# Sliding-window attention and Fourier mixing: crossbar transposes in one piece, crossbar transposes for four more chunks, and the masks of two head pairs moved from TensorE to VectorE

## The chip, the cores and the metric

The kernel runs on one core of a Trainium2 chip. The metric is the device time of one execution in microseconds (us), as the median of several runs.

The engines have these names in the profile: PE is TensorE (matrix multiply), PEld its weight loads, DVE is VectorE, ACT is ScalarE, POOL is GpSimd, and SP is SyncE, which here does nothing but issue DMAs. The crossbar is the way of a DMA that transposes 2-byte data from one place in the on-chip memory to another (`dma_start_transpose`).

## The reference

There are two stages. The first is attention over q, k, v of shape (batch 4, heads 8, sequence 768, head size 64). A query at position i sees the keys j with 0 <= i - j < 96 (the local band) and the 8 first keys (the global ones). Each score gets a bias that depends on head and distance:

```
scores = scale * q @ k.T
bias   = -slope[h] * dist          # dist = i - j in the band, 96 for the global keys
a      = softmax(where(keep, scores + bias, -1e9))
x      = a @ v                     # then heads side by side: (4, 768, 512)
```

The second stage mixes by Fourier transforms and ends in a two-layer network:

```
u   = x + real(fft(fft(x, axis=1), axis=2))
un  = (u - mean(u)) / sqrt(var(u) + 1e-6)
out = u + relu(un @ w_ch1) @ w_ch2      # w_ch1 512 x 2048, w_ch2 2048 x 512
```

## The kernel before

**Tiles.** Two heads are worked on together as a head pair `hp` (four a batch); `n = 4 * b + hp` counts head pairs over all batches, 0 to 15. The second stage works on chunks of 256 sequence rows: chunk `c = 3 * b + pr`, three a batch, twelve in all.

**Attention of a head pair.** q and k are loaded into `qs` or other staging tiles in fp32, cast to fp16 (`qk16`), and transposed to `TT` (profile name `qkT`), so that the head dimension lies on the partitions. In batches 0 and 1 TensorE transposes (`trans`, L527) and an engine copies the result out. In batches 2 and 3 (`b >= FB`) the crossbar does it (`trans_dma`, L499): four DMA transposes of 64 partitions by 768 elements each (L506), one for each half `a` of the partitions and each parity `t` of the position. The loads go through three `qs` buffers, so a load waits for the cast of the head pair before. q and k come with one DMA each, v with two, one for each parity (L343).

Then come three score units a head pair (`score`, L542, g = 0, 1, 2): 128 keys against the 256 queries that their band reaches, for two blocks of keys and both heads, so four matmuls with 64 rows each (L564). In batches 0 and 1 two matmuls ahead of them (L554, L559) put the bias and the mask into the accumulator: scaled identity `sid` times the distance table `dist`. ScalarE then writes the exponential straight to `ex` (L587). In batches 2 and 3 these two matmuls are left out: ScalarE writes the exponential to a buffer `er` (L584), and VectorE multiplies it by the mask `mk` = exp(-slope * dist) into `ex` (L599). The masks are made by ScalarE (L1309), two a head pair, after batch 1's attention. The global keys have their own matmuls (`glob`, L643), on keys gathered in `kG` by two small GpSimd copies a head pair (L493). `av` (L691) multiplies the exponentials with v, and VectorE normalizes.

**Between the stages.** x goes to DRAM and back in another row order (`bounce`: writes L730, read L738; ScalarE issues them for b > 0). VectorE folds x, `y_unit` (L892) and `u_unit` (L972) do the transforms by matmul, and GpSimd mirrors some results (L940).

**Second stage of a chunk.** u is scaled to fp16 `un` and transposed to `UNT` (profile name `unT`): for chunks 0 to 6 by TensorE (`nt_unit`, eight transposes at L1063, then one copy by ScalarE or VectorE, L1071 or L1073), for chunks 7 to 11 by the crossbar (`nt_dma`, L1043), two DMA transposes a chunk (L1048). There are two `unT` buffers: the transpose of chunk c waits until the ph of chunk c - 2 is done. ScalarE squares `un` in place once `unT` is there (L1031). `ph_unit` (L1091) is the first layer in 8 units a chunk (eight matmuls of 256 columns each), its relu by ScalarE or VectorE (L1097, L1098). `pg_unit` (L1114) is the second layer, eight groups of four matmuls a chunk for chunks 0 to 7; from chunk 8 on it is L1195 with fewer products.

**Order.** The class `Plan` writes the order of all instructions before the kernel runs. It keeps an estimated clock for each engine, estimated costs for each operation, and tokens for what each step needs. TensorE draws from four streams (`MIX` transforms and u transposes, `ATT` attention, `PH`, `PG`): it takes the unit that can start first by the estimates, in the first two streams from the next ten. Work of other engines is emitted when its estimated start comes, each with a rank. Each engine then executes its list strictly in that order; on SP one list holds loads, crossbar transposes and stores of results (L1128, L1269), and a transpose that waits for its input holds back what stands behind it. Score tiles in the accumulator memory come from a ring `xx` of two banks, and while batches 0 and 1 are worked on also from two banks `C` and `D`. These two are then given to the ph and pg rings: the token `("CD",)` opens the ph units when the last user of C and D is done. `BANKS(b)` says which rings a unit may use.

## Time and profile before

| what | us |
|---|---|
| median of 7 runs | 269.84 (269.17 to 271.75) |
| the profiled execution | 270.58 |
| its span, first to last instruction | 268.8 |
| outside of the span | 1.8 |
| mean granted TensorE clock | 0.999 |
| weights w_ch1, w_ch2 have landed; loads of batch 2 begin | 71.1 |
| first score matmul of batch 2 | 106.1 |
| first ph matmul; first ph of chunk 6 (batch 2) | 54.3; 171.4 |

How to read it: a row of the timeline gives the start in us from the first instruction, the duration, engine and line, what is written and what is read, the shapes and a count. Matmuls are pipelined and their ends are modelled, so that durations of neighbours overlap; what a group costs TensorE is the distance from its start to the start of the next group. A row of the waits gives the engine and line that waited, for whom, the total in us, how often, and the longest wait. The tenths of the span have 40 slices of 6.72 us, each digit the busy share in tenths.

Of the DMAs, the crossbar transposes for q and k are issued 32 times with a median of 1256 ns on SP and land 2.4 to 6.5 us after their issue (median 3.7). Those for u are issued 10 times, 1217 ns, and land 2.4 us after.

### The profile page before, as it was taken

The page shows a single profiled execution, that of the slowest core. Times are in us where ns is not written, and L with a number is a line of the kernel's source. Part 1 is how long each engine was busy: PE and PEld are TensorE (multiplying, and loading weights), DVE is VectorE, ACT ScalarE, POOL GpSimd, SP SyncE. Part 2 cuts the span into 40 slices and gives each one's busy share as a digit, 9 for nine tenths or more (in the row PEclk, how much of TensorE's full clock was granted, in tenths as well). Part 3 has the DMA queues.
Part 4 walks back from the last instruction along what each step waited for, and adds up shares of the span by engine and source line. Part 5 has one row for each costly group of instructions (what it writes and reads, how often), then busy time and mean ns, then how long its engine had stood idle before and what let it go on. Part 6 is the DMA issues. An engine that isn't in the chain of part 4 may idle for free.

```text
span 268.8 us, 6248 instructions
## 1 busy us (share of the span) xinstructions
PE 255.7 (95%) x2540; PEld 181.4 (67%) x2540; DVE 172.6 (64%) x349; ACT 151.2 (56%) x263; POOL 60.1 (22%) x127
## 2 busy tenths in 40 slices
PE   8899899999999899999999799999999999999994
PEld 3454558577855776676675356769777668888883
DVE  3566873833399475861559957878998645525473
ACT  1479693987536737993880354896443345444300
POOL 1442398143010152321200307101100511010000
PEclk9999999999999999999999999999999999999999
DMA  7999959999589975996898896402072241511122
GB/s 202 294 291 308 295 181 234 216 216 213 125 156 256 274 159 120 217 188 131 218 153 191 171 308 151 106 2 41 0 166 110 59 97 42 81 40 41 39 82 78
DMA packets 75743, 42.03 MB, mean 156 GB/s; under 512 B 32834, under 2 KB 71746, under 8 KB 75714
## 3 DMA queue, kind: packets, MB, share of 16 engines
q1 hardware_dynamic: 68658, 32.71, 51.6%
q0 software_dynamic: 4224, 4.19, 9.3%
q10 hardware_dynamic: 2832, 4.72, 7.3%
q8 instruction: 20, 0.33, 0.6%
q14 instruction: 9, 0.07, 0.1%
HBM read 31.92 MB, written 9.44 MB: 154 GB/s over the span
## 4 chain that ended last, share of the span: by engine, by line
PE 66%; DMA 20%; SPq 4%; DVE 3%; POOL 2%; ACT 2%; issue 1%; ACTq 0%; POOLq 0%
PE ph L1091 26%; PE pg L1114 12%; DMA w<-in_moe_w_ch_dram 10%; PE pgD L1195 5%; DMA qs<-in_q_dram 5%; PE sc L564 4%; PE py L892 4%; PE pgA L1195 4%; PE pav L691 3%; DMA u<-in_v_dram 3%; PE pu L972 3%; DMA qs<-in_v_dram 2%; PE sc L559 2%; SPq L506 2%; SPq L372 2%; PE pt L527 1%
## 5 line engine op out<-in xcount | busy, mean ns | idle before, releaser
L1091 PE MATMUL ph<-unT,w 128*128 128x256 f16 x768 | 94.1, 273 | 2.7 <-ACT hT L1097 1.6
L1091 PEld LDWEIGHTS <-w 128*128 128x128 f16 x768 | 72.7, 98 | 17.1 <-issue 6.2
L1097 ACT ACTIVATE hT<-ph 128x512 f16<-128x512 f32 x78 | 46.2, 596 | 41.5 <-PE ph L1091 41.4
L1114 PE MATMUL pg<-w,hT 128*128 128x512 f16 x256 | 60.7, 379 | 0.0
L1114 PEld LDWEIGHTS <-hT 128*128 128x128 f16 x256 | 24.2, 98 | 23.4 <-issue 0.6
L587 ACT ACTIVATE ex<-sc 128x992 f16<-128x992 f32 (+2 forms) x24 | 20.8, 924 | 8.4 <-PE sc L564 8.4
L584 ACT ACTIVATE er<-sc 128x992 f16<-128x992 f32 (+2 forms) x24 | 21.6, 922 | 3.7 <-PE sc L564 3.5
L376 ACT ACTIVATE qk<-qs 128x384 f16<-128x384 f32 (+1 forms) x29 | 13.8, 525 | 14.8 <-DMA qs<-in_q_dram 5.3
L1123 DVE SCALAR_TENSOR_TENSOR u<-pg,sm,u 128x512 f32<-128x512 f32 x16 | 12.0, 747 | 12.2 <-PE pg L1114 12.2
L1098 DVE TENSOR_SCALAR hT<-ph 128x512 f16<-128x512 f32 x18 | 12.4, 690 | 10.8 <-PE ph L1091 10.8
L466 POOL CAST v<-qs 128x768 f16<-128x768 f32 x8 | 6.8, 853 | 54.4 <-DMA qs<-in_v_dram 54.4
L564 PE MATMUL sc<-qkT 64*128 64x256 f16 (+1 forms) x192 | 17.0, 262 | 2.0 <-ACT er L584 1.6
L599 DVE TENSOR_TENSOR ex<-er,mk 128x992 f16<-128x992 f16 (+2 forms) x24 | 15.0, 627 | 3.7 <-ACT er L584 3.5
L691 PE MATMUL pav<-v,ex 128*128 128x65 f16 x352 | 16.3, 193 | 1.0 <-DVE x L711 0.7
L691 PEld LDWEIGHTS <-ex 128*128 128x128 f16 x352 | 15.2, 97 | 2.4 <-DVE x L711 0.9
L564 PEld LDWEIGHTS <-qkT 64*128 64x128 f16 x192 | 5.8, 94 | 16.2 <-issue 13.9
L991 DVE SCALAR_TENSOR_TENSOR u<-pu,xr 128x512 f32<-128x512 f32 x18 | 11.7, 689 | 5.5 <-PE pu L972 3.2
L907 ACT ACTIVATE zy<-py 128x1024 f16<-128x1024 f32 (+1 forms) x12 | 10.0, 844 | 9.2 <-PE py L892 6.6
L940 POOL COPY ww<-zy 128x512 f16<-128x512 f16 x16 | 9.9, 650 | 22.7 <-PE py L892 20.6
L1038 POOL TENSOR_SCALAR sm<-sm 128x2 f32<-128x2 f32 x12 | 2.3, 193 | 56.6 <-ACT un L1031 56.5
L1031 ACT ACTIVATE un<-un 128x512 f16<-128x512 f16 x24 | 14.9, 624 | 0.0
L1195 PEld LDWEIGHTS <-hT 128*128 128x128 f16 x128 | 12.5, 98 | 1.6
(129 smaller groups left out, 381.9 us busy)
## 6 DMA issues: line engine op xcount, KB each, us to landing
out_dram<-u SPq DMA_DIRECT2D x24, 256.0 KB, 2.4
w<-in_moe_w_ch_dram POOLq DMA_DIRECT2D x8, 512.0 KB, 19.5
qs<-in_q_dram SPq DMA_DIRECT2D x9, 384.0 KB, 5.9
qs<-in_k_dram SPq DMA_DIRECT2D x9, 384.0 KB, 6.4
qs<-in_v_dram SPq DMA_DIRECT2D x16, 192.0 KB, 4.8
xr<-xd ACTq DMA_DIRECT2D x3, 768.0 KB, 5.4
u<-in_v_dram SPq DMA_DIRECT2D x5, 384.0 KB, 6.9
w<-in_q_dram SPq DMA_DIRECT2D x4, 384.0 KB, 6.5
```

What stands on the lines that cost most here:

```text
L376: A(d, s, AF.Copy)
L564: nc.tensor.matmul(pa[:, s, c0:c0 + cw], TT[n][lo:lo + 64, 1, i * P:(i + 1) * P], TT[n][lo:lo + 64, 0, i * P:i * P + cw], start=(b > 1), s ...
L584: A(mine(), cut(pa), AF.Exp, 0.0, 0.125)
L587: A(cut(expst[hp][:, :, g * 512:g * 512 + (384 if g == 2 else 512)]), cut(pa), AF.Exp, 0.0, 0.125)
L599: VT(o, mine(), m, op=ALU.mult)
L691: nc.tensor.matmul(po[:, jj, hh * 65:(hh + 1) * 65], lhsT, v16[b % 2][:, i, h, 0:65], start=(jp == 0 and a == 0), stop=(a == len(ops) - 1) ...
L1031: A(x, x, AF.Square, accum_out=MV[c][:, a, 2:3])
L1091: nc.tensor.matmul(ph[:, a * CH:(a + 1) * CH], W1[0][:, d, jb * P:(jb + 1) * P], UNT[c][:, d, :], start=(d == 0), stop=(d == ND - 1))
L1097: pl.later([("ACT", act(512), lambda: A(dst, ph, AF.Relu)), ("DVE", dve(512), lambda: V.tensor_scalar_max(dst, ph, 0.0))], [], e, [("h", c ...
L1098: ("DVE", dve(512), lambda: V.tensor_scalar_max(dst, ph, 0.0))],
L1114: nc.tensor.matmul(pg, HT[c][:, jb, t * P:(t + 1) * P], W2[0][:, jb, :], start=(jb == 0), stop=(jb == NJ - 1))
L1195: nc.tensor.matmul(o, lhs(j), rhs(j), start=(first and j == 0), stop=(j == NK - 1), skip_group_check=True)
```

## The change

1. **q and k of batches 2 and 3 in one crossbar transfer.** The four transfers of a head pair become one of 128 partitions by 1536 elements. The layout of the cast (`qk16`) changes so that one copy of 768 columns makes it, in place of two of 384. k is now loaded with two DMAs, one for each parity, as v is; q keeps one. So k's transposed blocks come out in the order that the scores want, while q's stay interleaved. The scores and the global scores of batches 2 and 3 read q through strided views (`tile_of`): the moving operand comes in runs of 64 columns. Score blocks are 256 columns wide in place of 240.
2. **u by the crossbar for chunks 3 to 11**, in one transfer a chunk in place of two; chunks 0 to 2 stay on TensorE. The layout of `unT` changes so that ph reads two runs of 128 columns.
3. **Masks of head pairs 2 and 3 of batch 1 by VectorE** (`DM`). Their scores take the path of batches 2 and 3: no bias matmuls, exponential to `er`, product with `mk`. The masks of these two head pairs are made after batch 0's last exponential in place of after batch 1's attention. The casts of v in batches 0 and 1 get buffers of their own (`v0`), so that `er` is free for this.
4. **The planner.** TensorE's clock gets 0.1 us more when a unit of scores with 64 rows follows one of another kind, or the other way round (`narrow`). Units of batch 1 may use banks C and D only while more than `KEEP` = 4 uses of them are left. Estimated costs of loads, casts and transposes are adapted.

```diff
+    def pe(self, us, after=0.0, narrow=False):
+        if narrow != self.narrow:
+            us += 0.1
+        self.narrow = narrow
...
+    KEEP = 4
...
+                                 if g and self.rings[g] and not (g in ("C", "D") and (("CD",) in self.tok or
+                                                                  "" in ring and self.left[("CD",)][0] <= self.KEEP))]
...
+    DM = ((1, 2), (1, 3))
...
-                    if w < 2:
+                    if w < 1:
                         run_dma(t.rearrange("p (m t) d -> p m (t d)", t=2), src, b, h0)
                         return
...
-            for t in range(2):
-                copy_on(on, qk16[n][:, t, w], stage[("t", n, w)].rearrange("p (h i t) d -> p t i h d", h=2, t=2)[:, t])
+            copy_on(on, qk16[n][:, w].rearrange("p n t h d -> p (n t) h d"),
+                    stage[("t", n, w)].rearrange("p (h j) d -> p j h d", h=2))
...
-        return ("xx", "C", "D") if b < 2 else ("xx",)
+        return ("xx", "C", "D") + ("",) * b if b < 2 else ("xx",)
...
+    def tile_of(n, lo, w, i, nb=1):
+
+        x = TT[n][lo:lo + 64, w]
+        if n < FB * HP or w:
+            return x[:, i * P:i * P + P].rearrange("p (t m) -> p t m", t=2)
+        if nb == 1:
+            return x.rearrange("p (i t a m) -> p i a t m", t=2, a=2, m=64)[:, i // 2, i % 2]
+        if i % 2 == 0:
+            return x.rearrange("p (i t a m) -> p i a t m", t=2, a=2, m=64)[:, i // 2]
+        o = (i // 2) * 256 + 64
+        return x[:, o:o + 384].rearrange("p (y q m) -> p y q m", y=2, m=64)[:, :, 0:3:2]
...
-            o = TT[n].rearrange("p w (i a t m) -> p a t (w i) m", a=2, t=2, m=64)[:, a, t]
-            nc.sync.dma_start_transpose(o, qk16[n][64 * a:64 * a + 64, t].rearrange("p w i h d -> p (w i h d)"))
+            nc.sync.dma_start_transpose(TT[n].rearrange("p w (j x) -> p (w j) x", x=P),
+                                        qk16[n].rearrange("p w n t h d -> p (w n t h d)"))
...
+        pem = b < 2 and (b, hp) not in DM
...
-            if b < 2:
+            if pem:
                 for s in range(2):
                     lhsT = sid[:, 2 * hp + s, :]
...
+                    if b >= FB:
+                        nb = 1 if cw == P else 2
+                        o = pa[:, s, c0:c0 + nb * P]
+                        o = o.rearrange("p (y t m) -> p y t m", y=2, t=2) if nb == 2 else o.rearrange("p (t m) -> p t m", t=2)
+                        nc.tensor.matmul(o, TT[n][lo:lo + 64, 1, i * P:(i + 1) * P], tile_of(n, lo, 0, i, nb), start=True, stop=True)
+                        continue
...
-        for a in range(2):
-            def xb(a=a):
-                if a == 0:
-                    UNT[c] = buf("unT", c, [P, ND, CH], FP16, 1)
-                nc.sync.dma_start_transpose(UNT[c][:, :, a * P:(a + 1) * P], T[("un", c)][:, a])
+        def xb():
+            UNT[c] = buf("unT", c, [P, 2, ND, P], FP16, 1)
+            nc.sync.dma_start_transpose(UNT[c].rearrange("p a d m -> p (a d) m"), T[("un", c)].rearrange("p a f -> p (a f)"))
...
-        if c >= 7:
+        if c >= 3:
             return nt_dma(c)
...
-            pl.later([("ACT", 2 * act(NM), m)], [("c", "dist"), ("x", 1, 3, 2)], 0.0, [("mk", hp)], rank=3)
+            pl.later([("ACT", 2 * act(NM), m)], [("c", "dist")] + ([] if (0, hp) in DM else [("ex", 0, 3, 2)] if (1, hp) in DM else [("x", 1, 3, 2)]), 0.0, [("mk", hp)], rank=3)
```

## The prediction

> **What bounds the kernel now.** I read the page first: busy shares, then the tenths of the span, then the chain.
>
> ```profile
> PE 255.7 (95%) x2540; PEld 181.4 (67%) x2540; DVE 172.6 (64%) x349; ACT 151.2 (56%) x263; POOL 60.1 (22%) x127
> PE   8899899999999899999999799999999999999994
> PEclk9999999999999999999999999999999999999999
> PE 66%; DMA 20%; SPq 4%; DVE 3%; POOL 2%; ACT 2%; issue 1%; ACTq 0%; POOLq 0%
> ```
>
> TensorE is busy nearly everywhere, at the full clock, so no gain can come from the clock. Is it at its peak, too? In the timeline 32 matmuls of 256 columns start at 58.74 and the next group at 62.34: 112 ns each, and elsewhere 16 take 1.75 us, 109 ns. That is a stream of columns with no gaps. So from 56 us on, a microsecond of TensorE work removed is a microsecond of time, as long as TensorE always has something ready. The second view is therefore what TensorE waited for:
>
> ```profile
> PE ph L1091 <- ACT hT L1097: 1.6, 1, 1.6
> PE sc L564 <- ACT er L584: 1.6, 1, 1.6
> PE pz L1294 <- DVE eg L1291: 1.2, 1, 1.2
> PE ph L1091 <- ACT ex L587: 1.1, 1, 1.1
> ```
>
> Three waits lie past the start: 1.1 us at 53, 1.6 at 87, 1.6 at 153. Two of them are ScalarE standing in its own queue: at 80 to 85 and at 148 to 152 it waits to issue the read of the DRAM bounce (L738), and the evacuations behind that come late.
>
> **The masks (head pairs 2 and 3 of batch 1).** The timeline of TensorE, in us from the start:
>
> ```profile
> 47.66 0.49 PE L559 MATMUL sc<-dist,sid 128*128 128x384 f16 x2
> 48.08 0.34 PE L564 MATMUL sc<-qkT 64*128 64x256 f16 x4
> 48.35 0.59 PE L559 MATMUL sc<-dist,sid 128*128 128x496 f16 x2
> 48.87 0.39 PE L564 MATMUL sc<-qkT 64*128 64x256 f16 x4
> 49.22 1.05 PE L972 MATMUL pu<-t,ww 128*128 128x128 f16 x16
> ...
> 106.10 0.39 PE L564 MATMUL sc<-qkT 64*128 64x256 f16 x4
> 106.42 1.92 PE L1091 MATMUL ph<-unT,w 128*128 128x256 f16 x16
> ```
>
> With the bias, the first score unit takes 49.22 - 48.35 = 0.87 us; a unit without it (batch 2) 0.32, and the ph group ahead of it runs 0.09 longer (1.84 against 1.75): 0.41. Saved: 0.46. The same for the 960 form (0.81 against 0.31 + 0.09: 0.41) and the 768 form (0.69 against 0.27 + 0.09: 0.33). Sum 1.20 per head pair, **2.4 us of TensorE** for two.
>
> Added: six VectorE multiplies, 2 x (0.667 + 0.653 + 0.559) = 3.8 us by the rows of L599. VectorE is full from 46 to 53 but idle for 6.7 us in four gaps between 53 and 62, and the products are first read at 73 us (av of half 1). Without that cover they would hold the two er buffers and with them the score banks. ScalarE's exps stay (989 against 997 ns). Four masks of 0.72 us move from 80-88 us to just behind batch 0's last exp; ScalarE is idle for 4.8 us between 40 and 47. So both are costed at 0. Bound: if none of the masks fits, the ph start at 54 moves by 2.9 us.
>
> **The u transposes (chunks 3 to 6).** Eight transposes start at 101.64 and the next group at 102.08: 0.44 us a chunk, **1.8 us of TensorE** for four; also four evacuations of 0.69 to 1.01 us go. Added: four crossbar issues on SP. [...] I take 1.2 + 2.4 = 3.6 us a chunk, so 2.2 us later than now, up to 6 us where loads share the queue (L506's longest landing is 6.5). Chunks 3 to 5 have cover: at 97 us TensorE has 13 of 24 pg groups of batch 0 left, 0.86 us each. Chunk 6 has none of its own; see below. The squares on ScalarE wait for the landing as well, but the factor they feed is read at the end of the chunk's pg, over 10 us on.
>
> **Wider scores.** 48 more columns per row half and head pair, in paired matmuls: 0.02 us x 8, **+0.2 us**. The moving operand is now read in runs of 64. No row shows that; the nearest, L554, reads two separate runs and costs 370 ns for 480 columns beside 375 for 496 in one. I take 0; below nothing is excluded (no fewer columns), and half rate would be 24 units x 0.21 + 0.7 for pgl = +5.8.
>
> **SP and the DMA queues.** This step adds or removes no TensorE work; it decides whether the savings stay.
>
> ```profile
> 80.81 2.71 SPq L506 DMA_TRANSPOSE qkT<-qk  x1
> ...
> 87.59 1.56 SPq L506 DMA_TRANSPOSE qkT<-qk  x1
> ...
> 93.55 2.48 SPq L506 DMA_TRANSPOSE qkT<-qk  x1
> ...
> 97.47 5.22 SPq L506 DMA_TRANSPOSE qkT<-qk  x4
> ```
>
> In batch 2 the crossbar pieces of the first head pair are spread over 17 us, because SP serves them between loads and stores that wait; its first score runs only at 106.1. One issue replaces four. 32 issues of 1.26 us become 8; I take 1.3 us each, because L1048's 512 packets of 256 bytes take no longer than L506's 384; upper end 5.0, as now. Landing: 1536 packets x 24.5 ns (their mean in the trace) / 16 engines = 2.4 us in place of 0.6, so 3.7 + 1.8 = 5.5. The first pair is then ready near 80.8 + 1.3 + 5.5 = 88. Fewer u pieces for chunks 7 to 11: 5 issues less, hidden. Casts: one of 0.84 in place of two starting 0.47 apart (0.94 the pair), nothing.
>
> Against that: k loads go to 256-byte packets, 1536 x 24.5 in place of 768 x 32.1 ns, over 16: +0.8 us x 8 = 6.5 us of all engines; the u transfers add 4 x 1024 x 24.5 / 16 = 6.3. From 70 to 170 us the queues are already busy (packets, MB, share of 16 engines):
>
> ```profile
> q1 hardware_dynamic: 39570, 15.37, 71.0%
> q10 hardware_dynamic: 1888, 3.15, 13.7%
> ```
>
> 85% plus 13% is nearly full. k's second issue (0.65 us on SP) is paid by the 24 that go.
>
> How much must batch 2 gain? TensorE's reserve is the pg groups left over from batch 1:
>
> ```profile
> 168.33 1.89 PE L1114 MATMUL pg<-w,hT 128*128 128x512 f16 x8
> 170.06 1.06 PE L972 MATMUL pu<-t,ww 128*128 128x128 f16 x16
> ...
> 171.36 1.92 PE L1091 MATMUL ph<-unT,w 128*128 128x256 f16 x16
> ```
>
> The last reserve is used at 170, just when chunk 6 is ready. If TensorE gets there 2.4 + 1.3 = 3.7 us earlier and chunk 6's transpose is 2.2 later, batch 2 has to be **5.8 us earlier**, or the saving becomes a wait. Engine time needed before its last head pair is transposed: loads 4 x (1.5 + 2.35 + 2.35) = 25, transposes 4 x 2.35 = 9, and by the same packet means the bounce 7, two u chunks and four stores 6: 47, from 71 to 118. Now the last two pairs' kG copies run at 127.6. So the gain is about 9 us: enough, by 3.
>
> **Sum.** -2.4 - 1.8 + 0.2 = -4.0. Of the waits: the masks behind the bounce read at 86.6 (1.35 us of the chain ahead of the 1.6 us wait) are halved, and batch 1 leaves its last C/D banks sooner at 53, perhaps 1 us together; but SP and ScalarE still wait for bounces on fuller queues, so I book -0.6. Total -4.6. Against its own profiled execution: 270.58 - 4.6 = 266.0 (span 268.8 to 264.2); the median of seven, 269.84, lies 0.7 below that execution: **265.2**.
>
> **Rivals.**
> *More than the work* (0.20): batch 2 comes early enough that the waits at 87 and 153 go as well: -4.0 - 3.2 = 262.6. For: both are ScalarE behind a DMA that came later than planned. Against: the read stays in ScalarE's order.
> *The saving turns into a wait* (0.13): batch 2 is only 3 us earlier, TensorE waits 2.8 before chunk 6, the other waits stay: -4.0 + 2.8, 268.6. For: 98% full queues. Against: the 9 us above.
> *Slower* (0.13): SP holds batch 2 back. The u transfer of chunk 5 waits on SP for an unT buffer until ph of chunk 3 ends, as at 173.4, where SP stood 7.9 us; there no load stood behind it, at 104 to 114 the loads of batches 2 and 3 do. Each us that batch 2 comes later adds one. Against: SP is rid of 24 issues. It decides from a gain below 5.8 - 4.0 = 1.8 us; with batch 2 one us later than now, -4.0 + 6.8 = +2.8: 272.6.
> *It does not do what it says* (0.02): runs of 64 are read at half rate, +1.2 net: 271.0.
> The forecast has 0.52.
>
> **Numbers.** 265.2; its own case holds 263.6 to 267.0. The range 261.8 to 270.0 takes in the third case and most of the second. A measurement tells about 0.5% (1.35 us) from nothing. Faster: 0.52 + 0.20 + a third of the third case = 0.76; slower nearly all of the last two, 0.14; within 0.5% the rest, 0.10.
>
> **What would show it.** The bias matmuls L559 and L554 come 24 and 12 times in place of 32 and 16, the u transposes L1063 24 times in place of 56. L506 with 8 issues near 1.3 us; the first score of batch 2 before 95 us; the reserve of pg not empty when chunk 6's ph begins; waits of TensorE not above today's. I am wrong if SP shows a long wait for ph ahead of a load, if the transfers take 5 us to issue, or if sc matmuls without bias take over 0.35 us a unit.

## The result: slower, and its profile

The changed kernel takes 274.78 us (median of 12 executions, 271.58 to 278.34) beside 269.87 for the kernel before: ratio 1.0111, interval 1.0074 to 1.0148. The forecast was 265.2, with a range up to 270.0. (Each ratio here is to executions of the kernel before taken together with that run; ratios and intervals leave out executions more than 1.5 % above the fastest of their kernel, the medians don't.) The profiled execution of after took 273.68 us, span 271.9.

The same four lines of the page as before the change, now of the changed kernel:

```profile
PE 253.0 (93%) x2504; PEld 180.1 (66%) x2504; DVE 172.4 (63%) x349; ACT 149.5 (55%) x249; POOL 64.0 (24%) x127
PE   8899899699998879799988999999999999999994
PEclk9999999999999999999999999999999999999998
PE 53%; DMA 23%; SPq 8%; DVE 5%; POOL 4%; ACT 3%; issue 2%; ACTq 0%; POOLq 0%; DVEq 0%
```

TensorE is busy for 2.7 us less, but the span is 3.1 us longer: its share falls from 95 to 93 %, and in the chain that ended last from 66 to 53 %. The tenths show where: a 6 in slice 8 (48 to 54 us, where the moved masks are), and 7s and 8s in slices 13 to 17 and 21 to 22 (82 to 116 and 136 to 150 us). As a measure of TensorE's work I count 0.4167 ns for each column of each matmul (in the trace of before, pg matmuls of 512 columns, L1114, start 216 ns apart in the median and pu matmuls of 128 columns, L972, 56: 160 ns for 384 columns; the eight of one column, L1324 and after the change L1355, which start 13 ns apart, are counted as 64 columns, 0.2 us in all and the same for both kernels; the pairs of 64-row matmuls, which start 3 to 4 ns apart, are both counted). This column work is 246.49 us before and 242.84 after: 3.65 us are gone. What is left of the time from the first matmul to the last, the lost time, rose from 17.3 to 24.0 us. Gaps over 0.3 us past 40 us, by the same count, were 6.4 us before and are 12.5 now. What TensorE waited for:

```profile
PE ph L1122 <- ACT hT L1128: 3.9, 2, 2.2
PE sc L588 <- ACT er L610: 2.1, 1, 2.1
PE pu L1005 <- POOL rev L961: 1.7, 1, 1.7
PE pz L1325 <- DVE eg L1322: 1.2, 1, 1.2
PE sc L590 <- ACT unT L1102: 1.1, 1, 1.1
```

The wait near 153 is gone; new are those at 98, 108 and 142, and the one at 87 is still there. In place of 1.1 us at 53 there are now 1.1 at 51 and 0.8 at 52. None of the four from 87 on is for a DMA by name. They are for ScalarE or GpSimd, and one has to look at what these engines stood on. ScalarE and SP around 87 us:

```profile
86.40 0.84 ACT L384 ACTIVATE qk<-qs 128x768 f16<-128x768 f32 x1 [4.49 <-DMA qs<-in_q_dram]
87.01 0.36 ACTq L771 DMA_DIRECT2D xr<-xd  x1
87.67 0.84 ACT L384 ACTIVATE qk<-qs 128x768 f16<-128x768 f32 x1 [0.43 <-DMA qs<-in_k_dram]
88.42 1.06 ACT L1128 ACTIVATE hT<-ph 128x512 f16<-128x512 f32 x2
```
```profile
79.59 0.37 SPq L380 DMA_DIRECT2D qs<-in_q_dram  x1
80.07 3.02 SPq L351 DMA_DIRECT2D qs<-in_k_dram  x2
83.18 3.79 SPq L524 DMA_TRANSPOSE qkT<-qk  x1
87.03 0.57 SPq L1159 DMA_DIRECT2D out_dram<-u  x1
87.69 1.51 SPq L351 DMA_DIRECT2D qs<-in_v_dram  x2
```

ScalarE stands for 4.49 us before a cast of q whose load SP issued only at 79.59, and the evacuation hT (the copy of a ph result out of the accumulator memory), for which TensorE waits 1.7 us at 87, is behind it in ScalarE's order. SP meanwhile spends 3.79 us on one crossbar transfer (L524, the whole head pair). The loads of v behind it start at 87.69. GpSimd stands on those at 95, and with it the mirror rows that pu needs at 98:

```profile
95.49 0.82 POOL L474 CAST v<-qs 128x768 f16<-128x768 f32 x1 [5.88 <-DMA qs<-in_v_dram]
96.26 1.17 POOL L973 COPY ww<-zy 128x512 f16<-128x512 f16 x2
```

At 108.58 ScalarE has again stood 3.42 us on a cast of q (then sc waits 2.1 us for er), and at 143 it stood 3.51 us until it could issue the read of the bounce (then ph waits 2.2).

The parts of the change did what they say. Score units without bias, here of batch 1, take the time the prediction gave them, and batch 2's first score comes at 96.15 instead of 106.1:

```profile
50.13 0.39 PE L590 MATMUL sc<-qkT 64*128 64x256 f16 x4
...
96.15 0.39 PE L588 MATMUL sc<-qkT 64*128 64x256 f16 x4
96.48 1.92 PE L1122 MATMUL ph<-unT,w 128*128 128x256 f16 x16
```

The units with q in runs of 64 columns (L588) take what the plain ones (L590) take. But the queues from 70 to 170 us are nearly full (88.7 + 12.4 %; the share is the sum of the packets' times, which can overlap, so it can pass 100), and the eight whole transfers take SP 2154 to 5711 ns each, median 3262:

```profile
q1 hardware_dynamic: 50338, 16.00, 88.7%
q10 hardware_dynamic: 1888, 3.15, 12.4%
```
```profile
L524 SPq DMA_TRANSPOSE qkT<-qk x8: 2154/3262/5711, 83.2 to 153.9; - x8
```

### The profile page after: what moved, and what is told of

The parts are those of the page before. It is cut to its first block, busy times and chain, and to the rows that moved or that the text cites. A ratio compares the mean times of both kernels' runs of the same rounds, so it can differ in the third digit from the quotient of the medians.

```text
span 271.9 us, 6121 instructions
## 1 busy us (share of the span) xinstructions
PE 253.0 (93%) x2504; PEld 180.1 (66%) x2504; DVE 172.4 (63%) x349; ACT 149.5 (55%) x249; POOL 64.0 (24%) x127
## 4 chain that ended last, share of the span: by engine, by line
PE 53%; DMA 23%; SPq 8%; DVE 5%; POOL 4%; ACT 3%; issue 2%; ACTq 0%; POOLq 0%; DVEq 0%
PE ph L1122 20%; PE pg L1145 13%; DMA u<-in_v_dram 8%; SPq L380 6%; PE pgD L1226 5%; DMA qs<-in_v_dram 4%; PE pgA L1226 4%; DMA xd<-x 3%; PE pav L724 3%; DMA w<-in_q_dram 3%; DMA qs<-in_q_dram 2%; PE pu L1005 2%; PE py L925 2%; DMA qkT<-qk 1%; DMA qs<-in_k_dram 1%
## 5 line engine op out<-in xcount | busy, mean ns | idle before, releaser
L1128 ACT ACTIVATE hT<-ph 128x512 f16<-128x512 f32 x79 | 46.9, 597 | 48.5 <-PE ph L1122 44.7
L610 ACT ACTIVATE er<-sc 128x992 f16<-128x992 f32 (+2 forms) x30 | 27.4, 922 | 6.3 <-PE sc L588 5.7
L625 DVE TENSOR_TENSOR ex<-er,mk 128x992 f16<-128x992 f16 (+2 forms) x30 | 20.1, 669 | 15.1 <-ACT er L610 15.0
L384 ACT ACTIVATE qk<-qs 128x768 f16<-128x768 f32 x14 | 11.8, 844 | 16.7 <-DMA qs<-in_q_dram 10.4
L613 ACT ACTIVATE ex<-sc 128x992 f16<-128x992 f32 (+2 forms) x18 | 15.6, 926 | 6.7 <-PE sc L590 6.4
L1154 DVE SCALAR_TENSOR_TENSOR u<-pg,sm,u 128x512 f32<-128x512 f32 x16 | 11.9, 745 | 9.9 <-PE pg L1145 9.9
L1024 DVE SCALAR_TENSOR_TENSOR u<-pu,xr 128x512 f32<-128x512 f32 x18 | 11.7, 688 | 9.4 <-PE pu L1005 4.5
L1129 DVE TENSOR_SCALAR hT<-ph 128x512 f16<-128x512 f32 x17 | 11.7, 690 | 6.7 <-PE ph L1122 6.1
L513 POOL COPY kG<-qkT 64x8 f16<-64x8 f16 x32 | 9.7, 302 | 24.5 <-DMA qkT<-qk 20.6
L474 POOL CAST v<-qs 128x768 f16<-128x768 f32 x8 | 7.6, 954 | 30.3 <-DMA qs<-in_v_dram 30.3
L940 ACT ACTIVATE zy<-py 128x1024 f16<-128x1024 f32 (+1 forms) x11 | 9.4, 867 | 8.3 <-PE py L925 8.2
L1226 PEld LDWEIGHTS <-hT 128*128 128x128 f16 x128 | 12.5, 98 | 1.6
L942 DVE CAST zy<-py 128x512 f16<-128x512 f32 (+1 forms) x8 | 6.6, 824 | 10.8 <-PE py L925 6.7
```

The lines of the kernel that those rows point to most:

```text
L384: A(d, s, AF.Copy)
L610: A(mine(), cut(pa), AF.Exp, 0.0, 0.125)
L613: A(cut(expst[hp][:, :, g * 512:g * 512 + (384 if g == 2 else 512)]), cut(pa), AF.Exp, 0.0, 0.125)
L625: VT(o, mine(), m, op=ALU.mult)
L1128: pl.later([("ACT", act(512), lambda: A(dst, ph, AF.Relu)), ("DVE", dve(512), lambda: V.tensor_scalar_max(dst, ph, 0.0))], [], e, [("h", c ...
L1154: V.scalar_tensor_tensor(UT[c][:, t, :], pg, MV[c][:, t, 3:4], UT[c][:, t, :], op0=ALU.mult, op1=ALU.add)
```

## Three theories

The program's order of each engine is written by a planner that carries an estimated time for every landing. Comparing its times with the trace: of the loads of v for the second to seventh head pair of batches 2 and 3, the plan of before has the landings at 90.2, 98.9, 107.1, 116.3, 124.5, 131.1 us, and the casts start at 92.2, 100.5, 109.3, 117.4, 126.9, 133.0, one or two us late. After: planned 90.3, 100.6, 110.6, 120.9, 130.3, 139.1, started at 95.5, 106.7, 116.5, 127.2, 136.8, 147.1, five to eight us late. (The planned times come from running the kernels' own `Plan`. A late cast can also be a consequence of waits ahead of it, but the second pair's is 5.2 us late already.)

- **O, the order.** The written order supposes landings that come 5 to 8 us too early. Casts are put on ScalarE and GpSimd ahead of evacuations that TensorE needs, and the engines stand in order on them.
- **Q, the queues.** The DMA engines are simply too full; with any order TensorE would wait.
- **M, the masks.** VectorE's six multiplies and the moved masks of ScalarE hold up TensorE.

A fourth came up in the first experiment: **C, a collision** of the first crossbar transfer of a batch with the read of the bounce.

## Experiments

**Better estimates alone (e1).** The changed kernel with the planner's numbers nearer to its trace; the arithmetic is untouched.

```diff
-                pl.later([("SP", 0.55 if w < 1 else 1.1, run)], free("qs", i) + gate, 0.0, [("ld", n, w)], lat=1.7, dma=2.0 if w < 1 else 2.67)
+                pl.later([("SP", 0.55 if w < 1 else 1.6, run)], free("qs", i) + gate, 0.0, [("ld", n, w)], lat=3.0, dma=2.2 if w < 1 else 2.9)
...
-        pl.later([("SP", 1.3, xb)], [("qk", n, 0), ("qk", n, 1)] + free("qkT", n), 0.0, [("qkT", n)], [("free", "qk", n)],
-                 lat=3.0, dma=1.5)
+        pl.later([("SP", 3.5, xb)], [("qk", n, 0), ("qk", n, 1)] + free("qkT", n), 0.0, [("qkT", n)], [("free", "qk", n)],
+                 lat=3.5, dma=1.5)
...
-                     lat=1.7, dma=2.4 if b else 2.6)
+                     lat=4.5 if b else 1.7, dma=2.4 if b else 2.6)
```

> The changed kernel, with nothing altered but the planner's estimates: loads of batches 2 and 3 land later (issue 1.6 for 1.1 us, latency 3.0 for 1.7, queue time 2.2 and 2.9 for 2.0 and 2.67), the crossbar transfer costs SP 3.5 for 1.3 us, the bounce write lands 2.8 us later. Theory O (order): TensorE's extra waits between 96 and 144 us are ScalarE and GpSimd standing in their written order at casts whose loads land 5 to 8 us later than the planner supposed; with right landings the waits of over 0.3 us shrink from 12.5 us in sum to about 7, and the time falls by 4 to 6 us, to about 268. Theory Q (queues): the transfers themselves are too many for the queues, batch 2 and 3 arrive late whatever the order, and the time stays within 1.5 us of the changed kernel's 273.

Measured: 277.0, 277.37, 279.2 and, once, 267.99 us. The waits of TensorE in the profiled execution (277.0), and SP's queue:

```profile
PE sc L588 <- DMA qkT<-qk: 8.5, 1, 8.5
```
```profile
83.47 3.35 SPq L524 DMA_TRANSPOSE qkT<-qk  x1
86.92 0.58 SPq L1159 DMA_DIRECT2D out_dram<-u  x1
87.56 5.63 SPq L351 DMA_DIRECT2D qs<-in_v_dram  x2
93.29 4.49 SPq L380 DMA_DIRECT2D qs<-in_q_dram  x1
97.88 4.73 SPq L1159 DMA_DIRECT2D out_dram<-u  x1
```

The small waits have gone, but the transfer issued at 83.47 landed after 18.7 us; the transfer issued at 83.18 in the changed kernel had landed by 89. ScalarE had issued the read of the bounce at 84.11, 0.6 us after it. Of that read's 6144-byte packets, the six that started between 84 and 87 us took 3.1 us on average, the longest 5.75; in e11 below the longest takes 0.66, in the changed kernel 1.85. SP's issues from 87.6 on take 4.5 to 5.6 us a row. Then comes a thing that I had not thought of (columns: stretch, PE busy and count, PEld, DVE, ACT, POOL, granted clock of TensorE, DMA share, GB/s):

```profile
90.00:95.00 5.00, 3.69 (x42) 3.24 (x40) 1.55 (x2) 2.22 (x3) 1.39 (x2) 1.00 1.05 110
95.00:100.00 5.00, 0.00 (x0) 0.00 (x0) 0.00 (x0) 0.00 (x0) 0.00 (x0) 0.59 1.15 151
100.00:105.00 5.00, 2.77 (x15) 1.74 (x16) 2.90 (x7) 1.30 (x2) 2.64 (x7) 0.50 0.97 202
105.00:110.00 5.00, 5.00 (x55) 3.77 (x53) 2.93 (x8) 2.63 (x5) 3.14 (x7) 0.88 1.10 194
```

TensorE's wait lasts from 93.5 to 102.2. From 95.9 to 106.2, 10.24 us, its clock is at half; the last 3.9 us of that are work at half speed. So e1 decides nothing on O by its median. Its one good execution (268.0) is 3.6 us below the fastest of the changed kernel, but one execution proves little. That a collision with the read is what held the transfer up is only suggested by their closeness in time.

**Fewer small packets (e2).** k of batches 2 and 3 loaded in one DMA with 512-byte pieces, all else in the same written order. k's rows then lie in another order than the scores suppose.

```diff
-                    if w < 1:
+                    if w < 2:
```

> The changed kernel, in the same written order, but k is loaded with one DMA of 512-byte pieces in place of two of 256-byte pieces. (Its rows then lie in another order than the scores suppose, so the output is not the reference's; all instructions and sizes are otherwise the same.) Theory Q: 6 us of all engines' queue time go, loads land 2 to 4 us earlier in the middle of the kernel, and the time falls by 3 us or more, to 270 or below. Theory O gives a smaller gain, 1 to 2 us, since landings still come 3 us or more after their planned times. If the k packets do not matter: no change within 1 us.

Measured: 272.54 us (271.5 to 274.42), ratio 1.0123 (1.0064 to 1.0183). About 2 us below the changed kernel's median; by ratio it can't be told from it. Gaps past 40 us: 9.9 of the 12.5. If the small packets cost anything, it is not what is lost. Q is not the main part.

**u of chunks 3 to 6 back on TensorE (e3), no VectorE masks in batch 1 (e4).**

```diff
-        if c >= 3:
+        if c >= 7:
```
```diff
-    DM = ((1, 2), (1, 3))
+    DM = ()
```

> The changed kernel with the u transposes of chunks 3 to 6 back on TensorE (chunks 7 to 11 stay with the crossbar). 1.8 us of TensorE work come back; 6 us of queue time go. Theory Q: 2 to 3 us of waits go, net 0 to -1. Theory O: the crossbar of u is not what is late, so the time is 1 to 2 us longer, 274.5 or so, unless the order shifts.

> The changed kernel with no masks by VectorE in batch 1 (the bias matmuls of these two head pairs back on TensorE). 2.4 us of TensorE work come back. Theories O and Q: the waits of 96 to 144 us stay, so 2 us longer, about 275. Theory M (masks): ScalarE and VectorE between 46 and 57 us are overfull with the masks, and TensorE waits for them there about as long as it saves; then the time stays within 1 us.

Measured: e3 279.1 us (277.76 to 280.21), ratio 1.037 (1.030 to 1.0439); e4 277.7 (276.26 to 280.53), ratio 1.0289 (1.0233 to 1.0345). Both are worse than the whole change. Taking a part away, and with it the work that it adds elsewhere, doesn't give its loss back: the order is written anew each time and the waits appear in other places. e4's longest is at 87.5, 4.3 us, ph behind hT on ScalarE; e3's at 149.6, 3.2 us, py behind zy on ScalarE. M in its simple form falls with e4.

**Each part alone (e5 to e8).** The kernel before with the masks, with u, with the whole transfers (and the loads of k and the casts that belong to them), and with the planner's two rules alone. The cores of the edits (e5, with all that reads `DM` and the buffers `v0`; e6, with the one-piece transfer and unT's layout; e7, with the copy, `tile_of` and the loads of k; e8, with `narrow`):

```diff
+    DM = ((1, 2), (1, 3))
```
```diff
-        if c >= 7:
+        if c >= 3:
```
```diff
-            o = TT[n].rearrange("p w (i a t m) -> p a t (w i) m", a=2, t=2, m=64)[:, a, t]
-            nc.sync.dma_start_transpose(o, qk16[n][64 * a:64 * a + 64, t].rearrange("p w i h d -> p (w i h d)"))
+            nc.sync.dma_start_transpose(TT[n].rearrange("p w (j x) -> p (w j) x", x=P),
+                                        qk16[n].rearrange("p w n t h d -> p (w n t h d)"))
```
```diff
+    KEEP = 4
```

> The kernel before with part 3 alone (masks of head pairs 2 and 3 of batch 1 by VectorE, v casts in buffers of their own; planner as before). 2.4 us of TensorE work go and no transfer changes. If the lost time of the changed kernel comes with its transfers (order or queues), the saving shows: about 267.3, TensorE's waits over 0.3 us after 40 us near 6 as before. If the masks themselves make waits (theory M): 269.5 or more.

> The kernel before with part 2 alone (u of chunks 3 to 11 by the crossbar, one transfer a chunk). 1.8 us of TensorE work go, 6 us of queue time and four SP issues come. Queues and order: waits of 1 to 3 us come back, so 269 to 271; if the u transfers are harmless: 268.

> The kernel before with part 1 alone (one crossbar transfer a head pair, k in two DMAs of 256-byte pieces, strided q). TensorE work +0.2 us. If the transfers of this part, or the order that the planner makes of their estimates, are what costs: waits in the middle of the kernel grow by 4 to 6 us, 273 to 276, with stretches of half clock in some executions. If the part is harmless by itself: 269.5 within 1.

> The kernel before with part 4 alone (0.1 us for a switch to or from 64-row matmuls, the last four uses of banks C and D kept from batch 1). No work changes; 269.5 within 1.5 if the planner's changes are harmless; over 271 if reordering by itself makes waits.

Measured, with the column work of TensorE (246.49 before) and the gaps of the profiled execution (6.4 before) beside it:

| | median us (low to high) | ratio (interval) | column work | gaps past 40 us |
|---|---|---|---|---|
| e5 masks | 270.58 (266.77 to 276.39) | 0.9991 (0.996 to 1.0021) | 244.23 | 8.0 |
| e6 u | 274.43 (274.30 to 274.98) | 1.0127 (1.0065 to 1.0189) | 244.79 | 10.5 |
| e7 q and k | 274.78 (274.32 to 276.13) | 1.0141 (1.0083 to 1.0199) | 246.81 | 7.5 |
| e8 planner | 270.21 (269.39 to 271.58) | 1.0021 (0.9997 to 1.0044) | 246.49 | 5.0 |

Masks and u each remove the work that was forecast (2.3 of 2.4, 1.7 of 1.8) and gain nothing; the planner's rules do nothing. u and the whole transfers, alone, each cost 1.3 to 1.4 %. e6 does not fit O: its casts of v start only 1.6 to 3.4 us after the plan. Its last pg group before chunk 6 starts at 164.1, chunk 6's ph at 172.9 (171.4 before), and between 166 and 173 TensorE stands 4.0 us in four gaps, most of them on VectorE's u. That looks like the prediction's rival "The saving turns into a wait": the reserve ran out before chunk 6 was ready. No run tests it further. In e7 nearly the whole loss is one place; ScalarE there, and the clock:

```profile
82.95 0.35 ACTq L758 DMA_DIRECT2D xr<-xd  x1
83.49 0.72 ACT L1329 ACTIVATE mk<-dist 128x640 f16<-128x640 f16 x1
90.28 0.84 ACT L376 ACTIVATE qk<-qs 128x768 f16<-128x768 f32 x1 [6.07 <-DMA qs<-in_k_dram]
91.03 1.07 ACT L1117 ACTIVATE hT<-ph 128x512 f16<-128x512 f32 x2
```
```profile
90.00:95.00 5.00, 3.34 (x16) 2.38 (x16) 0.69 (x1) 3.21 (x5) 0.49 (x3) 0.67 1.00 248
```

SP issued that load of k at 85.47 and it landed at 90.28; ScalarE stood 6.07 us on it with hT behind; TensorE waited 4.2 us, then ran 3.41 us at half clock. This is O at its plainest: the crossbar transfer of that cast's head pair is issued only at 97.2.

**One more staging buffer (e9), casts of q and k away from ScalarE (e10).** Both on the changed kernel.

```diff
-    NBUF = {"hT": 3, "qk": 2, "qs": 3, "qkT": 4, ...
+    NBUF = {"hT": 3, "qk": 2, "qs": 4, "qkT": 4, ...
```
```diff
-        pl.later([("ACT", act(768), lambda: cast("ACT")), ("POOL", 0.87, lambda: cast("POOL"))],
+        pl.later([("POOL", 0.87, lambda: cast("POOL"))],
```

> The changed kernel with four staging buffers for the loads of q and k instead of three; nothing else by hand (the planner writes a new order from it). Theory O (the loads land 5 to 8 us after the time that the written order supposes, and ScalarE and GpSimd stand in order on them): a load can be issued one buffer earlier, so the casts on ScalarE near 84 to 87 and 105 to 108 find their data there, and the two waits of TensorE that follow them (1.9 at 87, 2.2 at 108) shrink; the time is 269 to 272. Theory Q (the 16 DMA engines are too full from 70 to 170): the earlier issue only lengthens the queue, the landings come as late as before, and the time stays at 273 to 275.

> The changed kernel with the casts of q and k of batches 2 and 3 on GpSimd alone, so that ScalarE never stands on a load of q or k. Theory O: the waits 'ph <- ACT hT' at 87 and 'sc <- ACT er' at 108 go (together 4.1 us in the profile of the changed kernel), and GpSimd, which is 49 % busy, takes 12 more casts of 0.9 us; 269 to 271, unless GpSimd's own in-order waits (pu <- POOL rev, 1.9 us at 98) grow by as much, and then 273. Theory Q: the wait goes to the scores that lack their transposed pair, 'sc <- DMA qkT' appears, and the time stays at 273 to 275.

Measured: e9 275.3 us (272.67 to 281.56), ratio 1.0153 (1.0091 to 1.0215): no gain; the waits at 87 and 108 are gone, but 3.5 us at 94.6 (pu behind zy on ScalarE) and 2.4 at 151.7 came in their place. e10 272.84 (269.76 to 275.2), ratio 1.0054 (1.0018 to 1.009): 2 us better than the change. The waits that it was meant to remove are gone and there is no gap over 0.7 us between 71 and 150 (GpSimd was 24 % busy in the changed kernel, not the 49 % of the expectation); then GpSimd stands in its own order and TensorE loses 4.36 us at once:

```profile
PE pu L1005 <- POOL rev L961: 4.2, 1, 4.2
```

That speaks for O: the loss follows the engine that holds the casts. One more buffer (e9), with an order whose casts of v still start 0.1 to 5.2 us late, doesn't help.

**The first transfer of a batch behind the read of the bounce (e11), and that with the better estimates (e12).** The planner may place the transfer of a batch's first head pair only after the read of the previous batch's bounce. This changes places in the written order and adds no wait on a semaphore. e12 has the three edits of e1 as well.

```diff
-        pl.later([("SP", 1.3, xb)], [("qk", n, 0), ("qk", n, 1)] + free("qkT", n), 0.0, [("qkT", n)], [("free", "qk", n)],
+        pl.later([("SP", 1.3, xb)], [("qk", n, 0), ("qk", n, 1)] + free("qkT", n) + [("xr", b - 1)] * (hp == 0), 0.0, [("qkT", n)], [("free", "qk", n)],
```

> The changed kernel in which the crossbar transfer of the first head pair of a batch waits for the read of the bounce of the batch before, so that the two are never in flight together; the planner's estimates are those of the changed kernel. If the collision of a crossbar transfer with the read costs something in the changed kernel too (in the run with other estimates it took 15 us), the stretch from 82 to 95 gets calmer and the time falls by 1 to 2 us, to 271 to 273. If not, the first pair comes 2 to 3 us later, which the scores of batch 2 (first at 96, pair there at 89) don't feel: 273 to 275, unchanged.

> The changed kernel with the planner's estimates set to what its trace shows (loads of q and k 2.2 and 2.9 us of DMA time and 3.0 us until they land, 3.5 us of SP for a whole crossbar transfer, 4.5 us until the read of the bounce lands) and with the transfer of the first pair behind the read of the bounce, so that the two can't collide as they did in the run with other estimates. Theory O: the written order then fits the landings, the in-order waits of ScalarE and GpSimd fall to those of before, TensorE's waits after 40 us fall from 12.5 to some 7, no stretch of half clock is left, and the time is 267 to 269 (one execution of the earlier run without the collision took 268.0). Theory Q: the order can't help, since the data isn't there; TensorE waits for the scores' operands instead, 272 to 275.

Measured: e11 269.16 us (267.4 to 273.99), ratio 0.9974 (0.9945 to 1.0003); **e12 267.0 us (266.19 to 268.31), ratio 0.988 (0.9852 to 0.9908)**, faster than both kernels. e12's column work is that of the changed kernel, 242.84; its lost time is 18.6 us in place of 24.0. What TensorE waits for in e12, and what the casts of q and k on ScalarE and on GpSimd waited for in the changed kernel and in e12 (the group's line: count, busy, mean ns, idle before):

```profile
PE ph L1122 <- DVE hT L1129: 1.6, 1, 1.6
PE pvp L445 <- POOL v L429: 1.4, 3, 0.8
PE pz L1325 <- DVE eg L1322: 1.2, 1, 1.2
```
```profile
L384 ACT ACTIVATE qk<-qs 128x768 f16<-128x768 f32 x14 | 11.8, 844 | 16.7 <-DMA qs<-in_q_dram 10.4 <-DMA qs<-in_k_dram 6.3
L388 POOL CAST qk<-qs 128x768 f16<-128x768 f32 x4 | 3.3, 825 | 4.0 <-DMA qs<-in_k_dram 2.2 <-PE sc L590 0.9 <-DMA qs<-in_q_dram 0.9
```
```profile
L384 ACT ACTIVATE qk<-qs 128x768 f16<-128x768 f32 x11 | 9.2, 838 | 2.4 <-POOL kG L513 1.4 <-DMA qs<-in_q_dram 1.0
L388 POOL CAST qk<-qs 128x768 f16<-128x768 f32 x7 | 5.9, 845 | 20.4 <-DMA qs<-in_k_dram 19.7 <-DMA qs<-in_q_dram 0.6
```

ScalarE stands on its casts for 2.4 us instead of 16.7. Three casts have moved to GpSimd, which now stands 20.4 us on casts of q and k instead of 4.0, in places where it costs TensorE little. The bytes are nearly the same (19.0 and 19.2 MB on the two queues between 70 and 170 us; 95.0 % of 16 engines, where the changed kernel has 101.1 %), and the data is there no earlier: the casts of v of the second to sixth pair start at 94.8, 105.5, 118.1, 130.2 and 136.0 us, beside 95.5, 106.7, 116.5, 127.2 and 136.8 in the changed kernel. What has changed is the plan, which now has these landings at 92.4, 105.9, 118.4, 128.6 and 137.7. So Q falls and O holds. How much of the gain comes from the casts' other engine is not separated.

**Is it only the estimates (e13)? Which parts pay now (e14, e15)?** e13 is the kernel before with e1's estimates of loads and bounce; e14 and e15 are e12 without the masks and with u of chunks 3 to 6 on TensorE (the edits of e4 and e3).

```diff
-                pl.later([("SP", 0.55 if w < 2 else 1.1, run)], free("qs", i) + gate, 0.0, [("ld", n, w)], lat=1.7, dma=2.67)
+                pl.later([("SP", 0.55 if w < 2 else 1.1, run)], free("qs", i) + gate, 0.0, [("ld", n, w)], lat=3.0, dma=2.9)
...
-                     lat=1.7, dma=2.4 if b else 2.6)
+                     lat=4.5 if b else 1.7, dma=2.4 if b else 2.6)
```

> The kernel before with the same correction of the planner's estimates that helped the changed kernel (3.0 us and 2.9 us of DMA time for a load of q or k instead of 1.7 and 2.67, 4.5 us until the read of the bounce lands instead of 1.7); its four-part crossbar transfers stay as they are. If the gain of the corrected changed kernel is the change's own, this stays at 269 to 271, since the order of before already fits its landings to 1 to 2 us. If it is only the estimates, this one gains 2 to 3 us too, 267 to 268.

> The corrected changed kernel (267.0 us) without the VectorE masks of batch 1: TensorE has 2.3 us more work. If work is what counts once the waits are gone, 269 to 270; if the masks' waits eat their work even now, 267.

> The corrected changed kernel (267.0 us) with u of chunks 3 to 6 transposed on TensorE again: 1.7 us more TensorE work, four transfers fewer. If work is what counts, 268.5 to 269; if the transfers' 3.6 us of latency before a chunk's first product costs as much as it saves, 267.

Measured: e13 270.92 us (269.24 to 271.52), ratio 1.0026 (1.0001 to 1.0052): the estimates give the kernel before nothing. **e14 265.69 (265.3 to 266.15), ratio 0.9846 (0.9804 to 0.9888)**: without the masks it is 1.3 us faster still by the medians (0.9 by the ratios, whose intervals overlap), though TensorE has 2.3 us more work (245.11). e15 269.96 (267.69 to 274.41), ratio 0.998 (0.9952 to 1.0007): u by the crossbar is worth 3.0 us by the medians (2.7 by the ratios), more than its 1.7 us of work; the rest may be the order, which is written anew here too. So M is true in another form: once the order fits, the masks of batch 1 eat what they save. e12's waits of TensorE from 40 to 75 us, where these masks are multiplied, and e14's:

```profile
PE pvp L445 <- POOL v L429: 1.1, 2, 0.8
PE sc L590 <- ACT unT L1102: 1.1, 1, 1.1
PE pgl L676 <- ACT er L610: 0.5, 1, 0.5
```
```profile
PE sc L579 <- ACT eg L689: 0.4, 1, 0.4
PE ptu L1094 <- DVE u L1033: 0.3, 1, 0.3
```

From 40 to 80 us TensorE does no columns for 3.5 us in e12 and for 1.0 in e14. The other 2.7 us of their difference in lost time (18.6 against 13.4) lie later, most of it between 120 and 140 us.

**The transfer by itself (e16).**

> Not the computation (the output is zeros): transfers by themselves on otherwise idle queues, each round joined before the next: a whole 128x1536 crossbar transfer, the same as four pieces, the 768 KB read of the bounce in packets of 6144 bytes on ScalarE's queue, a 384 KB load in pieces of 256 bytes, and pairs of them. If a crossbar transfer and the read hinder each other by themselves, the pair takes far longer than the two one after the other (alone some 4 and 4 us; together over 12). If the collision in the run with other estimates needed the full queues, the pair takes 4 to 8 us, the sum at most.

Rounds, each joined by VectorE before the next, of these four (W, P, R, L) and of sums of them:

```diff
+    def whole():
+        nc.sync.dma_start_transpose(TT, qk)
+    def pieces():
+        for n in range(4):
+            a, t = n // 2, n % 2
+            nc.sync.dma_start_transpose(TT[:, 6 * t:6 * t + 6, 64 * a:64 * a + 64], qk[64 * a:64 * a + 64, 768 * t:768 * t + 768])
+    def read():
+        nc.scalar.dma_start(XR, xd.rearrange("(m r) d -> m r d", r=6))
+    def load():
+        nc.sync.dma_start(L.rearrange("p (h r d) -> p h r d", h=2, r=6), lsrc[:, 0:2])
```

From issue to landing, us: W 3.6 to 3.7 (SP's issue 1.27 to 1.42); P 6.3 from the first issue to the last landing (four issues of 1.2); R 4.4 to 4.6, with an L beside it, because these rounds ran side by side; W behind an L 4.3 to 4.5, and its issue then takes 2.4 to 2.8; W with R 6.4 to 6.9, and R then 5.0 to 5.3 (in the rounds with all three W takes 5.2 to 6.9). In the last two of these no L stood ahead of W, only R, issued 1.2 to 1.4 us before on ScalarE's queue, and W's issue still took 2.84 and 2.40. The very first W stood behind four stores of 1.5 MB: its issue took 11.7 us and it landed after 15.4. SP's issues of W behind a load, then one behind an R alone, and VectorE's wait for a W beside an R:

```profile
117.70 2.38 SPq L53 DMA_TRANSPOSE tt<-qk  x1
122.48 0.37 SPq L67 DMA_DIRECT2D l<-in_q_dram  x1
122.94 2.79 SPq L53 DMA_TRANSPOSE tt<-qk  x1
...
160.67 2.84 SPq L53 DMA_TRANSPOSE tt<-qk  x1
```
```profile
89.24 0.17 DVE L72 COPY qk<-tt 128x8 f16<-128x8 f16 x1 [6.74 <-DMA tt<-qk]
```

So the pair takes less than the two one after the other (3.7 + 4.6), with no trace of 18 us. C is not a property of the pair alone. And in these rounds SP's time for a whole transfer doubles when one other transfer is under way ahead of it: 1.3 us alone, 2.4 to 2.8 behind a load or a read; in the changed kernel it is 3.3 in the median.

**The table of two by two (e17, e18).** Without masks, each correction alone.

e17 is e11 and e18 is e1, both with:

```diff
-    DM = ((1, 2), (1, 3))
+    DM = ()
```

> The changed kernel without the VectorE masks, the first transfer of a batch placed behind the read of the bounce in the written order, estimates as the change has them. If the place of that transfer carries the gain (with masks it gave 5.6 of the 7.8 us), the time falls from 277.7 to 267 to 269. If the estimates carry it here, it stays above 273.

> The changed kernel without the VectorE masks and with the corrected estimates, the first transfer of a batch free to go ahead of the read of the bounce. If that transfer and the read hinder each other whenever they are in flight together with the loads of that stretch, one transfer again takes over 10 us to land, TensorE waits for it over 4 us near 95 to 105, and the time is 272 or more. If the long transfer was a matter of that one order, the time is 265 to 268, as with both corrections.

Measured: e17 275.98 us (273.25 to 277.06), ratio 1.0217 (1.0147 to 1.0286): my expectation of 267 to 269 fails. e18 was 267.55 in its profiled execution and 279.68, 280.76 and 276.4 in the others. The whole table: medians in us; the idle time of ScalarE before its casts of q and k in the profile; and by how many us the casts of v of pairs 2 to 7 start after the plan's landing, on average:

| | neither | transfer later | estimates | both |
|---|---|---|---|---|
| with masks | 274.8; 16.7; 6.3 | 269.2; 10.0; 1.5 | 277.2, once 268.0; 3.6; 8.7 | 267.0; 2.4; 1.1 |
| without | 277.7; 11.9; 7.6 | 276.0; 11.4; 5.6 | 278.0, once 267.6; 3.9; -1.0 | 265.7; 2.5; -0.7 |

(In the third column the last two figures are of the profiled execution: with masks a long one, without masks the good one.) The third figure answers e17: with masks, the later transfer happened to give an order that fits; without, it did not. Over all 19 kernels that compute the whole, the median (for e18 its profiled execution) is 265.7 to 270.9 us where the casts are late by 2.7 us or less on average, with e6 (2.3 late, 274.4) as the one exception, and 272.5 to 279.1 where they are late by 3.4 or more.

The estimates are what takes ScalarE off its loads (3.9 at most, against 10 or more), in each row. (That idle time is no price by itself: the kernel before has 14.8 in its group, and e13 cut it to 6.0 for nothing. It costs where an evacuation for TensorE stands behind the cast.) But with the estimates alone three of four executions are some 10 us longer than the fourth, for one and the same program; with the transfer later as well, none of nine is. In the profiled good execution of e18 the transfer (83.17) and the read (84.93) are in flight together and all transfers land within 8.2 us; in that of e1 they are, too, and one takes 18.7. What makes the difference within one program stays open: only e1's long wait has been seen in a profile, and that the long executions of e18 have the same one is inferred from their times and their mean clocks (0.975 to 0.988, against 1.000).

## Why the prediction was wrong, step by step

- **TensorE's work: right.** -4.0 was forecast, -3.65 measured: masks 2.3 for 2.4, u 1.7 for 1.8. Strided q at full rate: right (0.39 us a unit, as with plain q). The rival "it does not do what it says" is out.
- **Batch 2 earlier: right in the main.** First score at 96.15 (said: before 95), the reserve of pg not empty at chunk 6, and the wait at 153 gone. The last pair's kG copies come at 121.0 in place of 127.6: 6.6 us earlier, where 9 were forecast and 5.8 needed. It did not help; in e12, the faster kernel, the first score comes only at 102.1.
- **The waits: the step that failed.** I booked -0.6 us and "waits of TensorE not above today's"; gaps past 40 us rose by 6.1, from 6.4 to 12.5, and the whole lost time by 6.7. Against -3.65 of work this leaves +3.0; the spans differ by 3.1. I had asked only whether batch 2's operands come early enough as a whole, which is a question on TensorE's reserve. I had not asked what each engine has in its order at the time when a load comes late. Casts need not be early, but whatever is written behind them on ScalarE and GpSimd waits with them, as e7's 6.07 us and the changed kernel's 4.49, 3.42 and 5.88 show. e12 removes it by new estimates and one new place.
- **SP: mis-sized.** "I take 1.3 us each" for a whole transfer; it took 3.3 (2.2 to 5.7). The row I took, L1048, was measured from 170 us on, where the queues had become emptier (DMA share 0.30 from 170 to 240 us, 0.86 from 70 to 170); e16 gives 1.3 on idle queues and 2.4 to 2.8 behind another transfer. The landing, 5.5, was right (median 5.8).
- **Full queues: seen, and drawn wrongly.** 98 % was in the text and I concluded that batch 2 has 3 us to spare. The loads of v came 5 to 8 us after the plan's time, before 1 to 2; that lateness is where the order broke.
- **Masks at 0: wrong in the end.** With waits elsewhere they seem to gain (e4 is slower than the change); with a fitting order they save nothing, and probably cost about 1 us net (e12 against e14). The cover I named for VectorE, its gaps between 53 and 62 us, did not settle it: e12 loses 2.5 us more than e14 between 40 and 80. The bound "if none of the masks fits ... 2.9 us" was near this.
- **u: right in sign, better than forecast** where the order fits (2.7 to 3.0 us, e15), worse than nothing alone (e6). The nine transfers, for which 1.2 + 2.4 us were taken from L1048, took 1.25 us to issue and landed after 3.1 (medians, L1079).
- **The rival "Slower"** had the sign, but not the mechanism: no transfer of u held SP back, and batch 2 did come earlier.
- **The clock.** "No gain can come from the clock" left out that a loss can. The profiled execution of the changed kernel ran at full clock but for its last 2 us; others of its executions did not. By mean clock: 271.6 to 273.7 us for the five at 0.997 to 1.000, 272.8 to 277.1 for the four at 0.994, and 277.1 to 278.3 for the three at 0.988 and 0.981. A stretch of 3.41 us at half clock, as in e7, lowers the mean by 3.41 x 0.5 / 272 = 0.006 and loses at most 1.7 us of work. For most of the seven others, which are up to 5 us above these five, half clock alone is not enough. Longer waits are likely, but none of these executions was profiled.

## What to carry to other kernels

Here in-order engines share casts of landing data with evacuations that TensorE needs, and the change that made loads later cost at the cast, not at the user of the data: near 87 us ScalarE stood 4.49 us before one cast, and TensorE waited 1.7 us for the evacuation behind it. In such a kernel, compare each landing with the time at which the written order expects it, before counting saved work. After a change of DMA sizes or issue counts, write the order anew with the measured landings; here that, with one transfer moved as well, turned +1.1 % into -1.2 %, and the part of the change that looked the surest (the masks) then turned out to save nothing. A saving on the engine that bounds is worth its size only if no wait is put in its place: here 3.65 us of work went and 6.7 us of lost time came.

## What the runs showed of the hardware

- **A wait can cost twice.** In some profiled executions TensorE's clock records go to 0.5 during or just after a wait: for 3.41 us with one of 4.35 us (e7), for 6.83 with 4.31 (e4), for 10.24 with 8.7 (e1, where 3.9 us of it were work at half speed: 16 ph matmuls from 102.77 to 106.16, 3.39 us, beside 1.74 from 88.49). The length of the wait alone does not tell: e15 went to half clock after gaps of 0.6, 1.3 and 0.3 us, and e17 with one of 3.62 us did not. What decides it was not shown.
- **A whole crossbar transfer's issue time differed with what was under way**: 1.3 us on idle queues, 2.4 to 2.8 behind one 384 KB load in 256-byte packets or a 768 KB read on the other queue, 11.7 behind four stores of 1.5 MB (e16), 2.2 to 5.7 in the changed kernel.
- **A crossbar transfer can take 18.7 us** when it and a read in 6144-byte packets are under way on full queues (e1, DMA share 0.95 to 1.28 from 80 to 95 us); on idle queues the pair takes 6.4 to 6.9 us (e16). The cause is open.
